# Batch 0 of a linear attention and MLP kernel: k and v with nine tokens to a partition, v cast on the core, products by quarters of the array

## The chip, the core and the metric

The kernel runs on one core of a Trainium2 chip. The core has TensorE (PE, with its weight loads listed apart as PEld), VectorE (DVE), ScalarE (ACT), GpSimd (POOL) and SyncE (SP, which here only issues DMAs). The metric is device time in microseconds (us); lower is better.

## What is computed

Eight batches of eight heads, 576 tokens, head size 64, all float32:

```
q_s = softmax(q, over the 64 features)
k_s = softmax(k, over the 576 tokens)
kv  = k_s^T v                      # 64 x 64 per head
x   = q_s kv                       # heads joined: 576 x 512 per batch
out = x + relu(norm(x) * g @ w1) @ w2      # norm: layer norm, w1 512 x 2048, w2 2048 x 512
```

## The kernel before

The order of all engines is written out by hand: instructions run on each engine in the order in which the program emits them. `first_batch` (L947) sets up batch 0. After it a list of main steps (TensorE's products of the MLP) is walked by `run` (L829); side work of other batches is hung in at a position counted in units of 512 columns of product, so `(2, ...)` comes after four main steps of weight 0.5.

Batches are handled one after the other: c = 0 with plain products (`mm1_part` L497 gives `ph`, `mm2_stream` L537 gives `pc`), c = 1 to 7 with a seven-product scheme (`prod1` L729, `prod` L574), and a ninth pass for the last 64 tokens of all batches. While batch c runs through the MLP, the attention of later batches is prepared beside it; their loads are issued by `load_batch` (L1067, on SP) and `load_behind` (L1057, on POOL).

Batch 0, before its first `ph` product, goes like this:

- Loads. SP issues two of q's four token groups (`load_q0`, L960) and then four DMAs of k, two heads each (L970). A partition holds six tokens of a head, so 576 tokens fill 96 partitions (`T0 = 6`, `P0 = 96`). POOL waits with a small copy into `gate` (L994) until q's first half has landed; then it issues three DMAs of v, which cast to bf16 on the way (L996), two of q's other half (L999), and the weights (L1003, L99, L103), later q and k of batch 1 (L121). The tiles that k and v of batch 0 use are handed on to later tiles: k's exps share a buffer with k of batch 1, v with `hs`.
- q. ScalarE takes exp of the first two token groups (`exp_qt` L206), VectorE sums, inverts and scales (`norm_q` L910), TensorE transposes (`eq_pT` L935, in `pe_T` L915) and VectorE copies the transposed tile `eqT` out of PSUM (L924).
- k. ScalarE takes exp pair by pair of heads (`exp_k0` L279). TensorE sums over tokens by six products with a column of ones (`z0_mm` L291), VectorE inverts (`recip_z` L301).
- kv. `kv0_mm` (L306) takes six 128-wide products for two heads at once, of which only the two diagonal 64 x 64 blocks are wanted. VectorE scales the result by the inverse sums, masks it with `diag` and sums each row (L312). The row sums, times -1/512, are spread over a 128 x 128 tile `mbc` by ScalarE (L317) or, for the last pair, VectorE (L321): it subtracts the mean of x when it is multiplied by `eqT`.
- x, transposed and with its mean taken off, comes straight from TensorE: `xT_mm` (L325) multiplies `kv_sb` and `mbc` by `eqT` for token groups 0 and 1; `xT_out` (L338) scales by g, on VectorE for columns 0 and 1, on ScalarE for 2 and 3.
- The third and fourth token groups take exp and transposing in between (L1029 to L1040: `eq_pT(0, 2)` copied by ScalarE, `eq_pT(0, 3)` by VectorE); their row sums are taken by `z_q` (L926, tile `zs`) after the first four `ph` products (L1102).

`warm` (L843) multiplies a zero tile, only to keep TensorE busy: 34 times at the start, 11 times between the two transposes.

Products on part of the array stand already in two places: `kv_pairs` (L347, k^T v of batches 1 to 7, output halves of 64 partitions) and the ninth pass (L395, 64 x 64 blocks in all four quarters).

Of the kernel before, what the change touches and what calls it, by code (L numbers as in the profile page):

```python
# [12 lines left out]
FP32 = mybir.dt.float32  # L13
# [7 lines left out]
def kernel(  # L21
# [31 lines left out]
    C9 = B  # L53
    FAST = 1
    CAST = (1, 2, 3)
    T0 = 6
    P0 = S // T0
    assert SR == 64 and B % 2 == 0

    const = ctx.enter_context(tc.tile_pool(name="const", bufs=1))  # L60
# [10 lines left out]

    ident = const.tile([P, P], BF16)
    eps_ln = const.tile([P, 1], FP32)
    gate = const.tile([P, 4], FP32)
# [4 lines left out]
    ones_w = const.tile([P, P], BF16)  # L79
    diag = const.tile([P, P], FP32)  # L80
    mbc = const.tile([P, NP, P], BF16)
# [9 lines left out]
    vr = const.tile([P, 2, H, VW], BF16)  # L91
    vm = const.tile([P, 2, T, H, VW], BF16)

    w1_src = moe_w_ch1.rearrange("(ko ki) n -> ki ko n", ki=P)
    w2_src = moe_w_ch2.rearrange("(ko ki) n -> ki ko n", ki=P)

# [180 lines left out]
    kvbox = {}  # L277

    def exp_k0(j):  # L279
        hs = slice(2 * j, 2 * j + 2)  # L280
        if j == 0:
            eks[0] = raw.tile([P, T0, H, D], BF16, tag="kt", name="ek0", bufs=1)
        nc.scalar.activation(
            eks[0][0:P0, :, hs, :].rearrange("p t h d -> p h t d"), raws[0][0][0:P0, hs], AF.Exp
        )

    def k0_mm(j, t):
        hs = slice(2 * j, 2 * j + 2)
        return eks[0][0:P0, t, hs, :], raws["v0"][0:P0, hs, t, :], P

    def z0_mm(j):  # L291

        if j == 0:
            kvbox["z0"] = mm_ps.tile([P, NP], FP32, tag="m", name="z0")
        for t in range(T0):
            nc.tensor.matmul(
                kvbox["z0"][:, j : j + 1], k0_mm(j, t)[0], ones[0:P0],
                start=(j == 0 and t == 0), stop=(t == T0 - 1), skip_group_check=True,
            )

    def recip_z():  # L301
        kvbox["rz"] = sml.tile([P, NP], FP32, tag="rzk", name="rzk")
        kvbox["sum"] = sml.tile([P, NP], FP32, tag="lnv", name="kvs")
        nc.vector.reciprocal(kvbox["rz"], kvbox["z0"])

    def kv0_mm(j):  # L306
        pool, tag = (att_ps, "a") if j < 2 else (mm_ps, "m")
        pkv = pool.tile([P, P], FP32, tag=tag, name="pkv")
        for t in range(T0):
            lhsT, rhs, w = k0_mm(j, t)  # L310
            nc.tensor.matmul(pkv[:, 0:w], lhsT, rhs, start=(t == 0), stop=(t == T0 - 1))
        nc.vector.scalar_tensor_tensor(  # L312
            kv_sb[:, 0, j, :], in0=pkv, scalar=kvbox["rz"][:, j : j + 1], in1=diag,
            op0=ALU.mult, op1=ALU.mult, accum_out=kvbox["sum"][:, j : j + 1],
        )
        if j < NP - 1:
            nc.scalar.activation(  # L317
                mbc[:, j], ones_w, AF.Copy, scale=kvbox["sum"][:, j : j + 1]
            )
        else:  # L320
            nc.vector.tensor_scalar_mul(  # L321
                out=mbc[:, j], in0=ones_w, scalar1=kvbox["sum"][:, j : j + 1]
            )

    def xT_mm(j, kh):  # L325

        if j == 0:
            pobox["T", kh] = mm_ps.tile([P, 2, 2, P], FP32, tag="m", name="pxT")
        ops = [(kv_sb[:, 0, j, :], j % 2)] if j // 2 == kh else []
        ops += [(mbc[:, j], i) for i in range(2)]  # L330
        for n, (lhsT, i) in enumerate(ops):
            nc.tensor.matmul(  # L332
                pobox["T", kh][:, i], lhsT, eqTs[0][:, 0:2, j, :],
                start=(j == 0 and n == 0), stop=(j == NP - 1 and n >= len(ops) - 2),
                skip_group_check=True,
            )

    def xT_out(i):  # L338
# [2 lines left out]
            nc.vector.tensor_scalar_mul(out=dst, in0=src, scalar1=g_one[:, i : i + 1])  # L341
        else:
            nc.scalar.activation(dst, src, AF.Copy, scale=g_one[:, i : i + 1])

    halves = (slice(0, 64), slice(64, P))

    def kv_pairs(b, ts=range(T + 1)):  # L347

# [586 lines left out]
    def eq_pT(c, t, eng):  # L935
        pe_T(eqTs[c], eqs[c][0][:, t].rearrange("p h d -> p (h d)"), t, eng)
# [10 lines left out]
    def first_batch():  # L947

        nc.scalar.preload_act_table_set("natural_log_exp_and_others")
        raws[0] = (  # L950
            mlp.tile([P, H, T0, D], FP32, tag="hT", name="kt0", bufs=1), None,
            raw.tile([P, H, T, D], FP32, tag="qt", name="qt"),
        )
        k0, _, q0 = raws[0]
        v0 = mlp.tile([P, H, T0, D], BF16, tag="hs", name="v0", bufs=1)
        raws["v0"] = v0
# [8 lines left out]
        def src0(x, h0, hn):  # L965
            return x[0, h0 : h0 + hn].rearrange("h (p t) d -> p h (t d)", t=T0)

        load_q0(0, 2, nc.sync)
        for h0 in range(0, H, 2):
            nc.sync.dma_start(  # L970
                k0[0:P0, h0 : h0 + 2].rearrange("p h t d -> p h (t d)"), src0(k, h0, 2)
            )
# [10 lines left out]
        nc.vector.memset(ones_w, -1.0 / DM)  # L983
        nc.vector.memset(diag, 0.0)
        for ps in halves:
            nc.vector.memset(diag[ps, ps], 1.0)
        nc.vector.memset(kv_sb[:, 1:B], 0.0)
        nc.vector.memset(vr, 0.0)
        for half in range(2):
            nc.vector.memset(vr[64 * half : 64 * half + 64, :, 4 * half : 4 * half + 4, D:], 1.0)  # L990
        nc.vector.memset(vm[:, :, :, :, D:], 1.0)
        make_identity(nc, ident)
        nc.gpsimd.tensor_copy(out=ident_f, in_=ident[0:KO1, 0:KO1])
        nc.gpsimd.tensor_copy(out=gate, in_=q0[:, 1, 0, 0:4])  # L994
        for h0, hn in ((0, 4), (4, 2), (6, 2)):
            nc.gpsimd.dma_start(  # L996
                v0[0:P0, h0 : h0 + hn].rearrange("p h t d -> p h (t d)"), src0(v, h0, hn)
            )
        for t in range(2, T):  # L999
            load_q0(t, 1, nc.gpsimd)  # L1000
        for kh in range(2):
            ks = slice(2 * kh, 2 * kh + 2)
            nc.gpsimd.dma_start(w1_sb[:, ks, 0:512], w1_src[:, ks, 0:512])  # L1003
        for nb in range(1, 4):
            load_w1(nb)
        load_w2(0)
        load_w2(1)

        new_eq(0)
        start_x(0)  # L1010
        warm(34)
        for t in range(2):
# [54 lines left out]
    def load_batch(b, parts=(2, 0), after=None):  # L1067

        alloc(b, parts)
        for which in parts:  # L1070
            if after is None:
                nc.vector.memset(raws[b][which][0:1, 0, 0, 0:1], 0.0)
            else:
                nc.gpsimd.tensor_copy(out=raws[b][which][0:1, 0, 0, 0:4], in_=after)
        for which in parts:
            hn = H // 2 if (b, which) == (B - 1, 2) else H
            for h0 in range(0, H, hn):
                load_main(nc.sync, b, which, h0, hn)
        if 0 in parts:
            load_krem(nc.sync, b)  # L1080
# [104 lines left out]
```

## Time and profile before

| what | us |
|---|---|
| median of 3 runs | 264.61 (262.91 to 264.71) |
| the profiled execution | 263.19 |
| its span, first to last instruction | 261.4 |
| granted TensorE clock in it | 0.999 of full |
| k of batch 0: last exp starts | 9.46 |
| first `ph` product starts | 15.17 |
| first `zs` product starts | 15.61 |

The profile is of one execution. Times in it count from the start of the span. "TENSOR_TENSOR eq<-eq,rq 128x512" is an instruction that writes tile eq from eq and rq; L913 is the line of the kernel. In the timeline and the chain the first number is the start and the second the duration; in square brackets stand the idle time before it and what ended that. In a table by stretches, each engine has its busy time and in brackets its count of instructions, then come granted clock, DMA share and GB/s. A DMA that casts is counted there by the bytes that it writes.

### The profile page before, as it was taken

How to read it: one execution, taken by the hardware profiler on the slowest of the kernel's cores; microseconds unless marked ns; L12 is line 12 of the kernel's file. 1: busy time of each engine (PE TensorE's matmuls, PEld its weight loads, DVE VectorE, ACT ScalarE, POOL GpSimd, SP SyncE). 2: the span in 40 equal slices, each digit the busy share in tenths (PEclk: the TensorE clock that was granted, in tenths of full speed). 3: DMA queues.
4: the chain of work that ended last, by engine and by line, in shares of the span. 5: the costliest groups of instructions: out<-in, count | busy, mean ns of one | idle time of the engine just before them, and what ended most of it. 6: DMA issues, size and time to landing. Idle time of an engine off the chain costs nothing.

```text
span 261.4 us, 6802 instructions
## 1 busy us (share of the span) xinstructions
PE 255.1 (98%) x2667; PEld 219.9 (84%) x2667; DVE 223.9 (86%) x505; ACT 176.7 (68%) x348; POOL 94.4 (36%) x148
## 2 busy tenths in 40 slices
PE   8899999999999999999999999999999999999993
PEld 6789755788888998899889889988898888888883
DVE  6778996989999999899889988998898979977873
ACT  4657780997887785789478947894789277538400
POOL 3962228414059205920881088009100800030000
PEclk9999999999999999999999999999999999999999
DMA  7999999989999994999399938995905323221014
GB/s 195 253 206 207 356 215 276 290 192 285 171 143 277 274 174 33 294 264 115 84 263 263 154 79 290 245 153 130 266 4 111 112 102 44 43 104 56 3 41 120
DMA packets 82616, 45.00 MB, mean 172 GB/s; under 512 B 58196, under 2 KB 79192, under 8 KB 82584
## 3 DMA queue, kind: packets, MB, share of 16 engines
q0 software_dynamic: 32464, 21.76, 44.9%
q1 hardware_dynamic: 49488, 22.29, 40.6%
q10 hardware_dynamic: 632, 0.53, 0.7%
q8 instruction: 20, 0.33, 0.5%
q14 instruction: 12, 0.10, 0.1%
HBM read 36.70 MB, written 9.44 MB: 177 GB/s over the span
## 4 chain that ended last, share of the span: by engine, by line
PE 92%; DMA 3%; DVE 2%; SPq 1%; ACT 0%; issue 0%
PE ba L589 21%; PE bx L742 20%; PE bb L742 10%; PE ph L505 8%; PE bb L589 5%; PE bc L589 5%; PE be L589 5%; PE pc L541 5%; PE bc L742 5%; PE po L404 3%; DMA kt<-in_k_dram 3%; PE pkv L361 2%; PE ptr L918 1%; PE pxT L332 1%; SPq L970 1%; DVE bb L773 0%
## 5 line engine op out<-in xcount | busy, mean ns | idle before, releaser
L589 PEld LDWEIGHTS <-hs 128*128 128x128 bf16 x512 | 49.8, 98 | 5.8
L742 PEld LDWEIGHTS <-w_raw 128*128 128x128 bf16 x480 | 45.5, 98 | 5.2
L259 POOL TENSOR_TENSOR tq<-xnT 128x256 bf16<-128x256 bf16 x26 | 16.8, 665 | 73.7 <-DMA xnT<-xn 49.5
L589 PEld LDWEIGHTS <-hT 128*128 128x128 bf16 x392 | 37.4, 98 | 4.2
L742 PEld LDWEIGHTS <-w1g 128*128 128x128 bf16 x360 | 34.3, 98 | 4.3 <-issue 0.3
L742 PE MATMUL bx<-tq,w_raw 128*128 128x256 bf16 x240 | 31.6, 273 | 0.0
L589 PE MATMUL ba<-w_q,hs 128*128 128x256 bf16 x256 | 30.8, 273 | 0.0
L766 ACT COPY bc<-bx 128x512 f32<-128x512 f32 x30 | 16.6, 594 | 19.0 <-PE bx L742 19.0
L773 DVE TENSOR_TENSOR bb<-bx,s 128x512 f32<-128x512 f32 x30 | 19.5, 694 | 8.2 <-ACT s L770 5.5
L607 POOL DMA_DIRECT2D out_dram<-ot x28 | 15.5, 559 | 23.7 <-DVE ot L601 23.6
L784 ACT ACTIVATE hT<-bb 128x512 bf16<-128x512 f32 x30 | 16.3, 595 | 10.8 <-PE bb L742 10.8
L417 ACT ACTIVATE scrap<-x,mv 128x512 bf16<-128x512 bf16 x32 | 23.1, 722 | 0.3
L784 ACT ACTIVATE hT<-bc 128x512 bf16<-128x512 f32 x30 | 16.3, 594 | 8.9 <-PE bc L742 8.9
L572 DVE TENSOR_TENSOR hs<-hT 128x1024 bf16<-128x1024 bf16 x32 | 21.7, 685 | 0.5 <-ACT hT L784 0.5
L404 PE MATMUL po<-kv_sb,eqT 128*128 128x128 bf16 x128 | 22.0, 219 | 0.0
L776 DVE TENSOR_TENSOR hT<-bx,s 128x512 bf16<-128x512 f32 x30 | 19.3, 683 | 3.1 <-PE bx L742 3.1
L449 DVE SCALAR_TENSOR_TENSOR x<-po,rq 128x512 bf16<-128x512 f32 x30 | 20.5, 683 | 0.9 <-PE po L404 0.8
L218 DVE TENSOR_REDUCE zq<-eq 128x16 f32<-128x1024 bf16 (+1 forms) x20 | 20.8, 1050 | 0.5 <-ACT eq L209 0.5
L615 ACT COPY s<-ba 128x512 f32<-128x512 f32 x15 | 8.8, 585 | 14.7 <-PE ba L589 9.7
L784 ACT ACTIVATE hT<-bx 128x512 bf16<-128x512 f32 x30 | 16.4, 602 | 0.7 <-PE bx L742 0.6
L589 PE MATMUL ba<-w_sb,hT 128*128 128x256 bf16 x128 | 16.6, 273 | 0.0
L770 ACT COPY s<-bb 128x512 f32<-128x512 f32 x30 | 16.6, 622 | 0.0
(157 smaller groups left out, 553.5 us busy)
## 6 DMA issues: line engine op xcount, KB each, us to landing
out_dram<-ot POOLq DMA_DIRECT2D x30, 256.0 KB, 6.4
kt<-in_k_dram SPq DMA_DIRECT2D x5, 1024.0 KB, 12.3
qt<-in_q_dram SPq DMA_DIRECT2D x4, 1024.0 KB, 5.9
qt<-in_q_dram POOLq DMA_DIRECT2D x2, 1024.0 KB, 12.5
kt<-in_k_dram POOLq DMA_DIRECT2D x2, 1024.0 KB, 13.7
vm<-in_v_dram POOLq DMA_DIRECT2D x16, 128.0 KB, 11.1
qt<-in_q_dram SPq DMA_DIRECT2D x3, 512.0 KB, 4.7
w_raw<-in_moe_w_ch_dram POOLq DMA_DIRECT2D x3, 512.0 KB, 10.3
```

Source lines behind the costliest of these rows:

```text
L218: nc.vector.reduce_sum(eqs[c][1][:, ts], eqs[c][0][:, ts], axis=AX.X)
L259: eng.tensor_tensor(out=dst[:, t], in0=x[:, t], in1=y[:, t], op=ALU.subtract)
L404: nc.tensor.matmul(pobox["p"][:, i * P : i * P + P], eqTs[c][:, t, i, :], kv_sb[:, c, i, :], start=True, stop=True,)
L417: nc.scalar.activation(scrap, x[:, t], AF.Square, bias=mv[:, t, 0:1], scale=-float(DM), accum_out=mv[:, t, 1:2],)
L449: nc.vector.scalar_tensor_tensor(x[:, t].rearrange("p (h d) -> p h d", h=H), in0=pobox[c, t].rearrange("p (h d) -> p h d", h=H), scalar=1. ...
L505: nc.tensor.matmul(ph[:, m % 2, at : at + tn], (w1g if c else w1_sb)[:, ko, m * P : (m + 1) * P], xnTs[c][:, t0 : t0 + tn, ko, :], start=( ...
L572: nc.vector.tensor_tensor(out=dst, in0=x, in1=y, op=op)
L589: nc.tensor.matmul(hbox[bank][:, t, cs], lhsT, rhs[:, cs], start=first and (own or t == 0) and k == 0, stop=k == KH - 1, skip_group_check= ...
L742: nc.tensor.matmul(dst[:, q], lhsT, rhs, start=first and q == 0 and ko == 0, stop=ko == 1, skip_group_check=True)
L773: nc.vector.tensor_tensor(out=at[g, "b"], in0=at[g, "x"], in1=at[g, "s"], op=ALU.add)
L776: nc.vector.tensor_tensor(out=h_out(g, 1, 1), in0=at[g, "x"], in1=at[g, "s"], op=ALU.add)
L784: nc.scalar.activation(h_out(g, odd, half), at[g, name], AF.Relu)
```

## The change

- k and v of batch 0 are laid out with nine tokens to a partition: a pair of heads takes 128 partitions, the lower 64 for the even head and the upper 64 for the odd one. A DMA of a pair has 128 runs of 2304 B.
- Both are loaded as float32 by SP, v right behind k, in four DMAs each; then SP loads q's other half in one DMA. POOL issues neither v nor q any more. VectorE casts v to bf16, pair by pair (`cast_v0`). The float32 v takes the second buffer of the tag that q of batches 0 and 1 uses.
- POOL's `gate` waits for k's last DMA instead of q's first. The zero fill of `kv_sb` for batches 1 to 7 moves from VectorE to POOL; VectorE fills that of batch 0.
- Sums and k^T v are taken by products on diagonal quarters of the array: 18 of 64 x 64 per pair for each, into two PSUM tiles. VectorE scales and sums the lower half, ScalarE the upper one. `diag`, `ones_w` and `mbc` go; VectorE makes one column `kvm` per pair, which `xT_mm` takes as a broadcast 128 x 128 operand.
- Four fill products come after each pair's sums (`warm(4)`), and the order of kv, xT and q's other half changes: `exp_qt` of groups 2 and 3 and both `eq_pT` now stand behind most of xT, and ScalarE's `xT_out` ahead of its copy of `eqT`.
- q and k of batches 6 and 7 are loaded in two halves each (before, only q of batch 7).

```diff
-    T0 = 6
-    P0 = S // T0
+    T0 = 9
...
+    ones_f = const.tile([P, D], FP32)
+    kvm = const.tile([P, NP], BF16)
...
     def exp_k0(j):
...
+            eks[0] = raw.tile([P, NP, T0, D], BF16, tag="kt", name="ek0", bufs=1)
+        nc.scalar.activation(eks[0][:, j], raws[0][0][:, j], AF.Exp)
...
+            kvbox["z0"] = [mm_ps.tile([P, NP], FP32, tag="m", name="z0") for _ in halves]
         for t in range(T0):
+            for z0, ps in zip(kvbox["z0"], halves):
+                nc.tensor.matmul(
+                    z0[ps, j : j + 1], eks[0][ps, j, t], ones[ps],
+                    start=(j == 0 and t == 0), stop=(t == T0 - 1), skip_group_check=True,
+                )
...
+        for z0, ps in zip(kvbox["z0"], halves):
+            nc.vector.reciprocal(kvbox["rz"][ps], z0[ps])
+
+    def cast_v0(j):
+        nc.vector.tensor_copy(out=raws["v0"][:, j], in_=raws["v0f"][:, j])
...
     def kv0_mm(j):
...
         for t in range(T0):
+            for pk, ps in zip(pkv, halves):
+                nc.tensor.matmul(
+                    pk[ps], eks[0][ps, j, t], raws["v0"][ps, j, t],
+                    start=(t == 0), stop=(t == T0 - 1),
+                )
+        rz, total = [kvbox[name][:, j : j + 1] for name in ("rz", "sum")]
+        lo, hi = halves
         nc.vector.scalar_tensor_tensor(
+            kv_sb[lo, 0, j, lo], in0=pkv[0][lo], scalar=rz[lo], in1=ones_f[lo],
+            op0=ALU.mult, op1=ALU.mult, accum_out=total[lo],
+        )
+        nc.scalar.activation(
+            kv_sb[hi, 0, j, hi], pkv[1][hi], AF.Copy, scale=rz[hi], accum_out=total[hi]
+        )
+        nc.vector.tensor_scalar_mul(out=kvm[:, j : j + 1], in0=total, scalar1=-1.0 / DM)
...
-        ops += [(mbc[:, j], i) for i in range(2)]
+        ops += [(kvm[:, j : j + 1].to_broadcast([P, P]), i) for i in range(2)]
...
+        def src0(x, j0, jn):
+            heads = x[0, 2 * j0 : 2 * (j0 + jn)]
+            return heads.rearrange("(j two) (s t) d -> (two s) j (t d)", two=2, t=T0)
...
         load_q0(0, 2, nc.sync)
+        for x, dst in ((k, k0), (v, v0f)):
+            for j in range(NP):
+                nc.sync.dma_start(
+                    dst[:, j : j + 1].rearrange("p j t d -> p j (t d)"), src0(x, j, 1)
+                )
+        load_q0(2, 2, nc.sync)
...
-        nc.vector.memset(kv_sb[:, 1:B], 0.0)
+        nc.vector.memset(kv_sb[:, 0], 0.0)
+        nc.gpsimd.memset(kv_sb[:, 1:B], 0.0)
+        nc.gpsimd.tensor_copy(out=gate, in_=k0[:, NP - 1, 0, 0:4])
...
         for j in range(NP):
             exp_k0(j)
             z0_mm(j)
+            cast_v0(j)
+            warm(4)
             if j == NP - 2:
                 g_columns()
         recip_z()
         kv0_mm(0)
         kv0_mm(1)
+        xT_mm(0, 0)
+        xT_mm(0, 1)
         kv0_mm(2)
-        xT_mm(0, 0)
+        xT_mm(1, 0)
+        xT_mm(1, 1)
         kv0_mm(3)
-        exp_qt(0, 2)
-        exp_qt(0, 3)
-        xT_mm(1, 0)
         xT_mm(2, 0)
-        xT_mm(0, 1)
+        xT_mm(2, 1)
         xT_mm(3, 0)
         xT_out(0)
         xT_out(1)
-        eq_pT(0, 2, nc.scalar)
-        xT_mm(1, 1)
-        xT_mm(2, 1)
-        eq_pT(0, 3, nc.vector)
+        exp_qt(0, 2)
+        exp_qt(0, 3)
         xT_mm(3, 1)
         xT_out(2)
         xT_out(3)
+        eq_pT(0, 2, nc.scalar)
+        eq_pT(0, 3, nc.vector)
...
-            hn = H // 2 if (b, which) == (B - 1, 2) else H
+            hn = H // 2 if b >= B - 2 else H
```

More of the change, by code (lines that the diff above doesn't have):

```diff
@@ L73 @@
     eps_ln = const.tile([P, 1], FP32)
-    gate = const.tile([P, 4], FP32)
     ones = const.tile([P, 1], BF16)
@@ L78 @@
     bones = const.tile([P, 2], BF16)
-    ones_w = const.tile([P, P], BF16)
-    diag = const.tile([P, P], FP32)
-    mbc = const.tile([P, NP, P], BF16)
+    ones_f = const.tile([P, D], FP32)
+    gate = const.tile([P, 4], FP32)
+    kvm = const.tile([P, NP], BF16)
     g_one = const.tile([P, KO1], FP32)
@@ L92 @@
     vm = const.tile([P, 2, T, H, VW], BF16)
+    halves = (slice(0, 64), slice(64, P))
     w1_src = moe_w_ch1.rearrange("(ko ki) n -> ki ko n", ki=P)
@@ L279, in exp_k0 @@
     def exp_k0(j):
-        hs = slice(2 * j, 2 * j + 2)
         if j == 0:
[L282 to L289, printed above, removed]
+            eks[0] = raw.tile([P, NP, T0, D], BF16, tag="kt", name="ek0", bufs=1)
+        nc.scalar.activation(eks[0][:, j], raws[0][0][:, j], AF.Exp)
     def z0_mm(j):
         if j == 0:
-            kvbox["z0"] = mm_ps.tile([P, NP], FP32, tag="m", name="z0")
+            kvbox["z0"] = [mm_ps.tile([P, NP], FP32, tag="m", name="z0") for _ in halves]
         for t in range(T0):
[L296 to L299, printed above, removed]
+            for z0, ps in zip(kvbox["z0"], halves):
[3 more added lines that the diff above has]
+                )
     def recip_z():
@@ L303, in recip_z @@
         kvbox["sum"] = sml.tile([P, NP], FP32, tag="lnv", name="kvs")
-        nc.vector.reciprocal(kvbox["rz"], kvbox["z0"])
+        for z0, ps in zip(kvbox["z0"], halves):
+            nc.vector.reciprocal(kvbox["rz"][ps], z0[ps])
+    def cast_v0(j):
+        nc.vector.tensor_copy(out=raws["v0"][:, j], in_=raws["v0f"][:, j])
     def kv0_mm(j):
-        pool, tag = (att_ps, "a") if j < 2 else (mm_ps, "m")
-        pkv = pool.tile([P, P], FP32, tag=tag, name="pkv")
+        pkv = [
+            pool.tile([P, D], FP32, tag=tag, name="pkv")
+            for pool, tag in ((att_ps, "a"), (mm_ps, "m"))
+        ]
         for t in range(T0):
-            lhsT, rhs, w = k0_mm(j, t)
-            nc.tensor.matmul(pkv[:, 0:w], lhsT, rhs, start=(t == 0), stop=(t == T0 - 1))
+            for pk, ps in zip(pkv, halves):
[5 more added lines that the diff above has]
+        lo, hi = halves
         nc.vector.scalar_tensor_tensor(
-            kv_sb[:, 0, j, :], in0=pkv, scalar=kvbox["rz"][:, j : j + 1], in1=diag,
-            op0=ALU.mult, op1=ALU.mult, accum_out=kvbox["sum"][:, j : j + 1],
-        )
[L316 to L323, printed above, removed]
+            kv_sb[lo, 0, j, lo], in0=pkv[0][lo], scalar=rz[lo], in1=ones_f[lo],
+            op0=ALU.mult, op1=ALU.mult, accum_out=total[lo],
+        )
+        nc.scalar.activation(
+            kv_sb[hi, 0, j, hi], pkv[1][hi], AF.Copy, scale=rz[hi], accum_out=total[hi]
+        )
+        nc.vector.tensor_scalar_mul(out=kvm[:, j : j + 1], in0=total, scalar1=-1.0 / DM)
     def xT_mm(j, kh):
@@ L343, in xT_out @@
             nc.scalar.activation(dst, src, AF.Copy, scale=g_one[:, i : i + 1])
-    halves = (slice(0, 64), slice(64, P))
     def kv_pairs(b, ts=range(T + 1)):
@@ L950, in first_batch @@
         raws[0] = (
-            mlp.tile([P, H, T0, D], FP32, tag="hT", name="kt0", bufs=1), None,
+            mlp.tile([P, NP, T0, D], FP32, tag="hT", name="kt0", bufs=1), None,
             raw.tile([P, H, T, D], FP32, tag="qt", name="qt"),
@@ L954, in first_batch @@
         k0, _, q0 = raws[0]
-        v0 = mlp.tile([P, H, T0, D], BF16, tag="hs", name="v0", bufs=1)
-        raws["v0"] = v0
+        v0 = mlp.tile([P, NP, T0, D], BF16, tag="hs", name="v0", bufs=1)
+        v0f = raw.tile([P, NP, T0, D], FP32, tag="qt", name="v0f")
+        raws["v0"], raws["v0f"] = v0, v0f
         def load_q0(t, tn, eng):
@@ L963, in load_q0 @@
             )
-        def src0(x, h0, hn):
-            return x[0, h0 : h0 + hn].rearrange("h (p t) d -> p h (t d)", t=T0)
+        def src0(x, j0, jn):
+            heads = x[0, 2 * j0 : 2 * (j0 + jn)]
+            return heads.rearrange("(j two) (s t) d -> (two s) j (t d)", two=2, t=T0)
         load_q0(0, 2, nc.sync)
[L969 to L972, printed above, removed]
+        for x, dst in ((k, k0), (v, v0f)):
[4 more added lines that the diff above has]
+        load_q0(2, 2, nc.sync)
         raws["g"] = outp.tile([KO1, P], FP32, tag="ot", name="g_rows")
@@ L982, in first_batch @@
         nc.vector.memset(bones[64:P, 1:2], 1.0)
[L983 to L986, printed above, removed]
-        nc.vector.memset(kv_sb[:, 1:B], 0.0)
+        nc.vector.memset(ones_f, 1.0)
+        nc.vector.memset(kv_sb[:, 0], 0.0)
+        make_identity(nc, ident)
+        nc.gpsimd.tensor_copy(out=ident_f, in_=ident[0:KO1, 0:KO1])
+        nc.gpsimd.memset(kv_sb[:, 1:B], 0.0)
+        nc.gpsimd.tensor_copy(out=gate, in_=k0[:, NP - 1, 0, 0:4])
         nc.vector.memset(vr, 0.0)
@@ L991, in first_batch @@
         nc.vector.memset(vm[:, :, :, :, D:], 1.0)
[L992 to L1000, printed above, removed]
         for kh in range(2):
```

## The prediction

> **What bounds the kernel now.** I read the page's busy shares and chain first, then the chain of waits over the first 45 us, then the timeline of the first 20 us, then the stretches of one us for the DMA rate.
>
> ```profile
> span 261.4 us, 6802 instructions
> PE 255.1 (98%) x2667; PEld 219.9 (84%) x2667; DVE 223.9 (86%) x505; ACT 176.7 (68%) x348; POOL 94.4 (36%) x148
> ...
> PE 92%; DMA 3%; DVE 2%; SPq 1%; ACT 0%; issue 0%
> ```
>
> TensorE is 98% busy and is 92% of the chain that ended last. The 3% of DMA is one piece, batch 0's k:
>
> ```profile
> 2.85 6.59 DMA kt<-in_k_dram
> ...
> 9.46 0.85 ACT ek L283
> ...
> 10.66 0.37 PE pkv L311 x6
> ...
> 13.62 0.39 PE pxT L332 x2
> ...
> 15.33 0.44 PE ph L505 x4
> 15.77 0.08 PE zs L930 x4
> ```
>
> Up to 15 us the chain goes from k's landing through exp, sums, k^T v and the folded product to the first `ph` product; from there TensorE leads almost alone (112 `ph` products take 11.37 us, later 16 take 1.75 us: 102 and 109 ns each). So nothing behind 15.6 us gives time back: what the first stage loses or wins reaches the end one for one. Three engines set that stage:
>
> ```profile
> 8.18 0.69 DVE L913 TENSOR_TENSOR eq<-eq,rq 128x512 bf16<-128x512 bf16 x1
> 8.93 0.40 PE L918 MATMUL ptr<-ident,eq 128*128 128x128 bf16 x4
> 9.36 0.42 DVE L924 COPY eqT<-ptr 128x512 bf16<-128x512 bf16 x1 [0.15 <-PE ptr L918]
> ...
> 14.27 0.59 ACT L920 COPY eqT<-ptr 128x512 bf16<-128x512 bf16 x1 [0.17 <-PE ptr L918]
> ...
> 15.37 0.84 ACT L343 ACTIVATE xnT<-pxT,g_one 128x256 bf16<-128x256 f32 x2 [0.51 <-PE pxT L332]
> ```
>
> VectorE's q chain (unchanged) holds TensorE until 8.93 and VectorE until 9.78. ScalarE makes q's transposed third quarter at 14.27, before its two `xnT` copies at 15.37. The rate of the loads:
>
> ```profile
> 3.00:4.00 1.00, 1.00 (x6) 0.69 (x5) 0.95 (x1) 0.00 (x0) 0.00 (x0) 1.00 1.13 340
> 4.00:5.00 1.00, 1.00 (x7) 0.71 (x5) 0.88 (x1) 0.00 (x0) 0.00 (x0) 1.00 1.15 368
> ...
> 6.00:7.00 1.00, 0.85 (x8) 0.51 (x6) 0.93 (x3) 0.92 (x2) 1.00 (x2) 1.00 1.09 264
> 7.00:8.00 1.00, 0.63 (x8) 0.60 (x9) 0.97 (x3) 0.79 (x1) 1.00 (x2) 1.00 1.08 256
> ```
>
> The last column is GB/s: 340 to 368 while q's 128 partitions arrive, 256 to 264 while k's 96 do.
>
> **The loads.** k becomes 128 partitions of 2304 B runs. Rate between 262 (k's now) and 368; I take 368, the row with 128 partitions in it. Counting bytes, q's first half is in by 4.06; exp then starts at 5.00, so a landing is seen 0.95 us after its last byte. k (1.18 MB, 3.2 us) is in by 7.3, seen 8.2 (now 9.46); v, now twice the bytes in SBUF, by 10.5, seen 11.4; q's other half (0.52 MB at 340) by 12.0, seen 13.0. At 262 v is seen at 14.0. SP's extra issues take 0.5 us each and end by about 6, ahead of the data: nothing. POOL loses v's 2.14 us and q's 1.88 us of issuing, but its gate now waits for k's last piece: w1 is issued from about 8.4 instead of 9.09. Its first product is now at 15.17, later below: nothing.
>
> **Moved setup.** The zero fill of kv_sb leaves VectorE (1.55 us at 2.40, in a stretch that ends in its wait for q at 5.66: no gain). On POOL it costs 1.55 (VectorE's row) to 5.7 us (28 times ident's 0.20); from 1.6 us on that ends before the gate opens. Later batches' halved loads are three more SP issues of 0.5 us, hidden since SP waits 14 us at a time for xn; if not, 0.5 us on a transpose.
>
> **VectorE's cast.** Four of 128x576 f32 to bf16. No such row: 0.24 each by the 128x1024 bf16 copy (0.43), 0.75 by the f32 clamp (0.68 for 512). I take 0.46, from the 0.42 of the 512-wide copy, nearest in size and not f32-slow. In order behind 9.78: three casts, g's two small ops (0.31), the last cast: 11.9 (13.1 at 0.75). TensorE's sums come later (below), so the casts are hidden; at 262 GB/s the last v makes it 14.5, and they aren't.
>
> **Quarter products.** 18 per pair of heads for z and 18 for k^T v instead of 6 each. Cheapest row: C9's 64x64 products, 32 in 0.38 us, 12 ns. Dearest: today's z, 18 in 0.59, 33 ns. Nearest, since two tiles of the array take turns: kv_pairs, 40 in 0.76, 19 ns. Entering and leaving them costs something too:
>
> ```profile
> 81.64 0.76 PE pkv L361 x40
> 82.40 1.85 PE bx L742 x16
> ...
> 108.94 1.75 PE bx L742 x16
> ```
>
> The 16 products behind them took 0.10 more. So a group of 18 is 0.34 + 0.10 = 0.44 (0.22 to 0.70). Fill: four products of 0.109 = 0.44 per pair; three of these lie before the last z.
>
> [...]
>
> **TensorE's timeline.** It is free at 9.16. Four z groups 1.76, three fills 1.31, g 0.2: 12.43, read at 12.55. (All exps of k are done by then.) Two reciprocals at 0.18: 12.9. Last fill and kv0(0): 13.31, readable 13.46. Each pair then needs ScalarE's scaled half (0.31 by the rows of L343 and L317, read of the accumulator 0.20) and VectorE's kvm (0.15 by its one-column row), 0.05 of signals: 0.7 us, against 0.37 + 0.41 to 0.50 now. xT(0) ends at 14.64; kv0(2) 15.08; xT(1), five products, 15.63; kv0(3) 16.07, readable 16.22; xT(2) 16.62; kvm(3) is ready at 16.93, xT(3) 16.97 to 17.52. Its first product is now at 13.62: 3.35 later.
>
> **The new order on ScalarE.** After its half of pair 3 (16.73) come both exps of q (1.15 by the pair at 5.00: 17.88), then both xT_out (0.84: 18.74), only then the copy of eqT (0.59: 19.33). TensorE, in order, transposes by 18.15, does four `ph` (18.2 to 18.65, now 15.17) and waits for that copy: zs at 19.4, now 15.61. **Sum: 3.8 us later**, and `ph` behind it follows.
>
> The profiled execution took 263.19 us (span 261.4, 1.8 around it), 1.4 below the median of 264.61 shown. 263.2 + 3.8 = 267.0; on the median 268.4; I forecast between, 267.8.
>
> **Rivals.**
> - Cheap products: 12 ns, no switching, casts of 0.35. z ends at 11.5, kv0(3) is readable at 14.5, ScalarE's row from 14.95 ends at 17.5: 1.9 us later, 265.8. For: C9's rows. Against: there four tiles take turns, here two.
> - Dear products or late v. At 33 ns with 0.10 switching, z ends at 13.5, kv0(3) is readable at 18.1, zs at 21.4: 5.8 later, 269.7. v at 262 GB/s: last cast 14.5, first scaling 14.9 instead of 13.46: 5.2 later, 269.1. For: z's row now; k's rate now. Against: kv_pairs; 340 to 368 with 128 partitions.
> [...]
> - Not slower: the landing of k is the only gate. k is seen 1.2 to 1.5 us earlier; if all behind it kept today's distance (9.46 to 15.17), the time would be 262.6. It decides if z, cast and kv0 are done 1.4 us behind k's last piece, as now. Against: v's last byte is 3.2 us behind k's, and VectorE is not free for casts before 9.78. Faster still would need a gain behind 15 us, where no row waits for what changes.
>
> **How the numbers follow.** Forecast (2.7 to 4.9 later) 0.54; cheap products 0.20; dear products or late v 0.13; drains 0.05; not slower 0.08. Leaving out a tenth at either end: from 264.5 (between not slower and cheap products) to 270.6 (dear ends on the median). Within 1% (2.65 us, about what a measurement of this kernel tells from no change) lie cheap products, most of not slower and a little of the forecast: 0.30; faster by over 1%: 0.05; slower: 0.65.
>
> **What would show it.** Right: z's last product near 12.4, the reciprocals behind TensorE rather than behind the cast, zs near 19.4 waiting for ScalarE's eqT copy, and later stages unchanged in length. Wrong in a step: groups of 18 far from 0.44; the last cast ending after z; k seen at 9.4 still; a granted clock under 1.00 or warm products over 109 ns in the stage. A time at or below 264 would refute the one-for-one passage to the end, or the timeline.

## The result, and the profile after

The changed kernel takes 267.13 us (median of 4 runs, 267.1 to 267.83); the kernel before, run beside it, 264.56 (4 runs, 262.91 to 264.71). The ratio is 1.0118, with a 95% interval of 1.0075 to 1.0161: slower by about 1.2%. The forecast was 267.8, with a range of 264.5 to 270.6. The profiled execution took 267.17 us, 3.98 more than that of before (263.19); its span grew by 4.0, from 261.4 to 265.4, and the granted clock is 0.999 in both. Two of the 87 executions of the kernel before that stand beside the experiments below, with spans of 264.5 and 265.3, count as slow and are left out.

The page's head of the kernel after, with its busy shares:

```profile
span 265.4 us, 7047 instructions
...
PE 258.7 (97%) x2776; PEld 221.8 (84%) x2779; DVE 223.7 (84%) x510; ACT 176.1 (66%) x353; POOL 93.6 (35%) x144
```

TensorE is still the bound, and is busy for 3.6 us more than before. The difference has to be looked for in the chain (start, duration, engine and tile):

```profile
9.28 0.37 PE z L289 x18
9.66 0.54 PE warm L846 x4
...
13.26 0.45 PE pkv L311 x18
...
18.11 0.84 ACT xnT L344 x2
18.95 0.48 ACT eqT L919
...
19.48 0.27 PE zs L929 x4
...
46.00 0.76 PE pkv L360 x40
...
260.88 0.46 PE bf L588 x8
```

What the reader is to see: from 9.28 on the chain is no longer k's landing but TensorE itself: sums and fill by turns, four times 0.91 us with g's product (0.31) ahead of the last. From 13.26 to 18.11 the chain goes to and fro between TensorE and the scaling of `kv_sb` and `kvm` on ScalarE and VectorE. It ends in ScalarE's two `xnT` and its `eqT` copy, and `zs` starts at 19.48 instead of 15.61, 3.87 later. In the kernel before, the last two of these rows stand at

```profile
42.12 0.76 PE pkv L361 x40
...
256.89 0.46 PE bf L589 x8
```

so the distance is 3.88 at 46 us and 3.99 at the end: 240 us of kernel behind the first stage add 0.1 us. All of the difference between these two executions is made before 19.5 us.

From the timeline of the kernel after (in brackets the idle time before, and what ended it), the landing of k as POOL's gate sees it, the last cast with g's copy ahead of it, and the reciprocals:

```profile
8.00 0.19 POOL L991 COPY gate<-kt 128x4 f32<-128x4 f32 x1 [3.43 <-DMA kt<-in_k_dram]
...
12.38 0.16 DVE L943 COPY g_one<-gcp 128x4 f32<-128x4 f32 x1 [0.85 <-PE gcp L942]
12.53 0.48 DVE L301 CAST v<-v0f 128x576 bf16<-128x576 f32 x1
12.93 0.37 DVE L298 RECIPROCAL rzk<-z 64x4 f32<-64x4 f32 x2
```

k is there at 8.00 where it used to be seen at 9.46, and nothing comes of it: its last sums are ready 4.7 us later. The stretches of 6 to 8 us show why it came early (the last column is GB/s):

```profile
6.00:7.00 1.00, 0.96 (x9) 0.60 (x7) 0.93 (x3) 1.00 (x3) 0.00 (x0) 1.00 1.07 401
7.00:8.00 1.00, 0.67 (x9) 0.63 (x9) 0.97 (x3) 0.94 (x3) 0.00 (x0) 1.00 1.04 387
```

With k on 128 partitions the loads run at 387 to 401 GB/s, where they ran at 256 to 264 with 96. These two executions lie far apart: over all profiles, the stretch from 6 to 7 us has 264 to 306 with 96 partitions (six profiles) and 320 to 401 with 128 (eight).

### The profile page after: what moved, and what is told of

Read it like the earlier page. It is cut to its first block, busy times and chain, and to the rows that moved or that the text cites. A ratio compares the mean times of both kernels' runs of the same rounds, so it can differ in the third digit from the quotient of the medians.

```text
span 265.4 us, 7047 instructions
## 1 busy us (share of the span) xinstructions
PE 258.7 (97%) x2776; PEld 221.8 (84%) x2779; DVE 223.7 (84%) x510; ACT 176.1 (66%) x353; POOL 93.6 (35%) x144
## 4 chain that ended last, share of the span: by engine, by line
PE 94%; DMA 2%; DVE 1%; ACT 1%; issue 0%; DVEq 0%
PE ba L588 21%; PE bx L741 20%; PE bb L741 10%; PE ph L504 7%; PE bb L588 5%; PE bc L588 5%; PE be L588 5%; PE pc L540 5%; PE bc L741 5%; PE po L403 3%; PE pkv L360 2%; DMA qt<-in_q_dram 2%; PE ptr L917 1%; PE warm L846 1%; PE pxT L333 1%; PE z L289 1%
## 5 line engine op out<-in xcount | busy, mean ns | idle before, releaser
L772 DVE TENSOR_TENSOR bb<-bx,s 128x512 f32<-128x512 f32 x30 | 19.4, 694 | 8.6 <-ACT s L769 5.6
## 6 DMA issues: line engine op xcount, KB each, us to landing
kt<-in_k_dram SPq DMA_DIRECT2D x3, 1024.0 KB, 11.7
```

The costliest lines, as they stand in the source:

```text
L772: nc.vector.tensor_tensor(out=at[g, "b"], in0=at[g, "x"], in1=at[g, "s"], op=ALU.add)
```

## The experiments

Each kernel ran beside the kernel before on the same chip. Its span is compared with the 265.2 to 265.4 of the changed kernel's runs, or with the spans of before, whose spread is a question of its own below. Spans are used because the time around them varies (1.7 to 3.2 us). Where the start of `zs` is compared, it is its start in the timeline; in a chain the same products can stand up to 0.2 us later, because the pieces of a chain don't overlap.

### The fill products left out

```diff
             cast_v0(j)
-            warm(4)
```

> The changed kernel without the four fill products after each pair's sums. Theory (the fill lies on TensorE's path): z's last product ends near 11.0 instead of 12.7, and then VectorE's last cast, near 12.3, sets the reciprocals; the first scaling starts at 12.7 instead of 13.7, zs at 18.5 instead of 19.48, span about 1.0 us shorter (264.4). Rival 1 (the fill fills idle time; v's landing or its cast sets the stage already): span within 0.2 us of 265.4. Rival 2 (without fill the clock falls): warm or ph products over 109 ns and a longer span.

Measured: 266.55 us (265.17 to 267.45, 10 runs), 1.0098 of before (1.0070 to 1.0125). Three of the ten executions, at a full clock, have spans of 263.4 to 263.8, 1.6 to 2.0 below the changed kernel, more than the 1.0 expected. In the other seven the mean clock is 0.985 to 0.994 and the span 264.6 to 265.7. The profiled one is of these. (Its casts took 455 ns in the median, not 619, and the last one waited for v's landing at 11.27. Shorter casts may be why the gain is larger than expected where the clock holds; no profile at a full clock shows it.) Its stretches, in which the third number from the right is the granted clock:

```profile
11.00:11.50 0.50, 0.48 (x31) 0.36 (x24) 0.39 (x4) 0.00 (x0) 0.50 (x2) 1.00 1.15 291
11.50:12.00 0.50, 0.00 (x0) 0.00 (x0) 0.47 (x3) 0.00 (x0) 0.50 (x1) 0.69 1.26 282
12.00:12.50 0.50, 0.00 (x0) 0.00 (x0) 0.33 (x3) 0.35 (x3) 0.50 (x2) 0.50 1.20 205
```

The clock is halved from about 11.7 to 18.5 us. A mean of 0.69 over 11.50 to 12.00 puts the fall near 11.7, when TensorE had been idle for some 0.2 us, after 2.3 us of quarter products with g's product among them. So the first five `pxT` products take 1.25 us (0.80 in the changed kernel), and `zs` comes half a microsecond later than with the fill:

```profile
12.60 1.25 PE pxT L333 x5
...
19.93 0.27 PE zs L929 x4
```

The theory and the second rival are both borne out: the fill stands on the path, and without it the mean clock is lower in seven of ten executions, which takes most of the gain back. In the profiled execution TensorE's whole idle stretch was about 1.1 us (11.47 to 12.60), and the clock fell at the beginning of it. Whether the quarter products ahead of it or the idle time brought the clock down, no run shows.

### Half of the fill

```diff
-            warm(4)
+            warm(2)
```

> The changed kernel with two fill products per pair instead of four. Theory (each fill product takes its 0.11 us of TensorE's path until VectorE's last cast sets the stage, and the clock holds while TensorE has work): 8 products fewer, of which 0.65 to 0.9 us show: zs near 18.7, span near 264.5, granted clock 1.00. Rival (the clock needs all four): clock under 0.997 in some executions, as without any fill, and a spread of over 1 us.

Measured: 266.84 us (266.15 to 267.68, 4 runs), 1.0113 (1.0073 to 1.0154). The chain of the profiled execution, which kept its clock:

```profile
18.62 0.27 PE zs L929 x4
```

`zs` is 0.86 earlier: four groups of 0.32 instead of 0.54. The span, 264.4, is 1.0 shorter. The fill is on the path product for product. In two of the four executions the mean clock was 0.993 and 0.994 and the spans 265.4 and 265.9, so half of the fill doesn't hold the clock safely.

### ScalarE's copy of eqT ahead of its last two xT

```diff
+        eq_pT(0, 2, nc.scalar)
         xT_mm(3, 1)
         xT_out(2)
         xT_out(3)
-        eq_pT(0, 2, nc.scalar)
         eq_pT(0, 3, nc.vector)
```

> The changed kernel with the transposes of q's third quarter and ScalarE's copy of them ahead of ScalarE's two xT_out. Theory (the order on ScalarE makes zs wait): zs starts near 18.75 instead of 19.48 and the span is 0.7 us shorter (264.7). Rival (the wait only moves: xT_out comes later and the second half of the first ph products waits instead): zs earlier but span within 0.2 us of 265.4.

Measured: 266.89 us (266.32 to 267.82, 4 runs), 1.0110 (1.0068 to 1.0152); spans of 264.4 to 264.8, some 0.8 below the changed kernel. The end of the stage in the timeline:

```profile
18.50 0.60 PE L504 MATMUL ph<-xnT,w_raw 128*128 128x256 bf16 x4
18.93 0.24 PE L929 MATMUL zs<-bones,eqT 128*128 128x2 bf16 x4
```

`zs` no longer waits for ScalarE; it comes when TensorE gets there, 0.55 earlier, and the `pkv` group at 46.00 comes 0.55 earlier too (45.45). The forecast 18.75 was missed by 0.18, of which 0.1 is that TensorE entered `pkv` at 13.36 instead of 13.26. The step was real and small: a seventh of the 3.87 at `zs`, a fifth of the loss by the spans.

### The fill in the kernel before

```diff
             z0_mm(j)
+            warm(4)
```

> The kernel before with four fill products after each pair's sums: one part of the change alone. Theory (fill lies on TensorE's path unless a wait covers it): z's last group ends at about 11.3 instead of 10.66, covered only in part by the wait for k until 10.36; zs 0.6 to 0.9 us later than 15.61, span 262.0 to 262.3. Rival (covered by the wait for k): span 261.4 as before.

Measured: 264.7 us (264.5 to 264.91, 10 runs), 1.0029 (1.0011 to 1.0047). The profiled span is 262.8, 1.4 over the profiled one of before, where 0.6 to 0.9 was expected:

```profile
11.53 0.46 PE warm L847 x4
11.99 0.35 PE pkv L311 x6
```

The expectation had forgotten the last fill: it stands ahead of the first `pkv`, which now starts at 11.99 instead of 10.66. `zs` came at 17.12, 1.51 later. So the fill alone, without a new layout, carries over a third of the loss.

### q's other half late, in the kernel before

```diff
         kv0_mm(3)
-        exp_qt(0, 2)
-        exp_qt(0, 3)
...
-        eq_pT(0, 2, nc.scalar)
         xT_mm(1, 1)
         xT_mm(2, 1)
-        eq_pT(0, 3, nc.vector)
+        exp_qt(0, 2)
+        exp_qt(0, 3)
         xT_mm(3, 1)
         xT_out(2)
         xT_out(3)
+        eq_pT(0, 2, nc.scalar)
+        eq_pT(0, 3, nc.vector)
```

> The kernel before with the changed kernel's place for q's other half alone: both exps behind the last xT but one, both transposes and ScalarE's copy of eqT behind ScalarE's two xT_out. Theory (the order on ScalarE costs by itself): zs starts 0.6 to 0.9 us later than 15.61, at 16.2 to 16.5, and the span grows as much. Rival (in the kernel before, q lands too late for an earlier place to matter): zs within 0.2 us of 15.61.

Measured: 264.94 us (263.32 to 266.33, 10 runs), 1.0036 (1.0006 to 1.0067). Its timeline:

```profile
15.47 0.60 PE L505 MATMUL ph<-xnT,w_raw 128*128 128x256 bf16 x4
...
16.60 0.25 PE L930 MATMUL zs<-bones,eqT 128*128 128x2 bf16 x4 [0.52 <-ACT eqT L920]
```

`zs` waits for ScalarE's copy as in the changed kernel and starts 0.99 later than before, just past the expected 16.2 to 16.5. But this execution also has v landing at 11.82, behind which `pkv` waited. The first `ph` starts 0.30 later than before (15.17); from there to `zs` it is 1.13 instead of 0.44. So about 0.3 of the 0.99 is v's lateness and about 0.7 the order's, as expected. The span, 263.5, is 2.1 over the profiled one of before: 0.94 of it is there when VectorE starts its last write (258.32, before 257.38), the rest lies behind that write. The spans run from 261.4 to 264.5, with a median about 1.2 over that of before on the same chip.

### The loads of later batches as before

```diff
-            hn = H // 2 if b >= B - 2 else H
+            hn = H // 2 if (b, which) == (B - 1, 2) else H
```

> The changed kernel with q and k of batches 6 and 7 loaded as before (only q of batch 7 in halves). Theory (hidden): span 265.2 to 265.4 as in the changed kernel, the stages of the last three batches unchanged in length. Rival (the halves delay SP's transposes or bring exps forward): a difference of 0.5 us or more in those stages.

Measured: 268.05 us (267.78 to 268.68, 4 runs), 1.0161 (1.0123 to 1.0199); spans of 265.4 to 265.5 and `zs` at 19.54. The spans are those of the changed kernel, so the halved loads are hidden, as the prediction had it; the higher median lies in the time around the span.

### No fill, and v cast by ScalarE

```diff
     def cast_v0(j):
-        nc.vector.tensor_copy(out=raws["v0"][:, j], in_=raws["v0f"][:, j])
+        nc.scalar.copy(raws["v0"][:, j], raws["v0f"][:, j])
...
             z0_mm(j)
-            cast_v0(j)
-            warm(4)
...
+        for j in range(NP):
+            cast_v0(j)
         recip_z()
```

> The changed kernel without fill and with v cast by ScalarE after k's exps instead of by VectorE. Theory (without fill VectorE's casts are the next limit): reciprocals end near 11.4, ScalarE's first half starts near 11.7 (behind its last cast), zs at 17.4 and the span 2.0 us shorter than 265.4. Rival (TensorE's products alone set it): same as without fill alone. Rival (v lands late): ScalarE waits for v and the first scaling starts after 12.5.

Measured: 265.32 us (264.97 to 267.64, 10 runs), 1.0068 (1.0039 to 1.0098); six executions at a full clock have spans of 263.2 to 263.6, the others, at 0.985 to 0.994, 264.3 to 265.9. The profiled one came as expected, `zs` at 17.41:

```profile
10.97 0.63 ACT v L301
...
17.41 0.27 PE zs L929 x4
```

With the fill gone and VectorE free, v's landing at 10.94 leads the chain. ScalarE's row of two exps, two `xnT` and the copy then sets the end, the row that the prediction named. About half of the loss is given back. v's last piece now comes 1.5 us behind the time at which k used to be there; how the rest is shared between that and ScalarE's row, this run doesn't show.

### A new order around the same layout

Sums of three pairs take the place of the 11 warm products between q's transposes, with two fill products behind each. Two casts and the last go to ScalarE, one stays on VectorE. The scaling is parted from the products (`kv0_out`), q's exps come right behind the last of it, and VectorE makes both copies of `eqT`.

```diff
         eq_pT(0, 0, nc.vector)
-        warm(11)
-        eq_pT(0, 1, nc.vector)
-        for j in range(NP):
+        for j in range(3):
             exp_k0(j)
             z0_mm(j)
-            cast_v0(j)
-            warm(4)
-            if j == NP - 2:
-                g_columns()
+            warm(2)
+        eq_pT(0, 1, nc.vector)
+        exp_k0(3)
+        cast_v0(0, nc.scalar)
+        cast_v0(1, nc.scalar)
+        z0_mm(3)
...
+        kv0_out(3)
+        exp_qt(0, 2)
+        exp_qt(0, 3)
...
+        eq_pT(0, 2, nc.vector)
         xT_out(2)
         xT_out(3)
-        eq_pT(0, 2, nc.scalar)
         eq_pT(0, 3, nc.vector)
```

> The changed kernel's loads and quarter products in another order: z of three pairs takes the place of the fill between the two transposes of q, two casts of v go to ScalarE after k's exps and one behind VectorE's first scaling, products of k^T v stand ahead of their scaling, q's other half before the last xT, its copies on VectorE; four fill products per pair become two in four places. Theory (the layout is not what costs: the place of z, fill, casts and copies is): z ends near 9.6, the reciprocals near 10.1, kv0(3) waits for v's last piece (10.9) and its cast, ph starts near 14.3 and zs near 14.8, both about 0.8 us earlier than in the kernel before; span 260.5 to 261.0 with the clock at 1.00. Rival (the layout costs by its later v): ph starts after 15.2 and the span is not below 261.4. Rival (clock): falls in some executions, spans of 262 and more.

Measured: 264.12 us (263.8 to 265.13, 12 runs), 1.0002 (0.9978 to 1.0026); spans of 262.0 to 263.3. `zs` came at 16.55, and the expected 14.8 was missed by 1.75 us. Three groups of sums with fill took 2.10 us (7.89 to 9.99), where the 11 warm products had taken 1.20, so q's second transpose slipped from 8.93 to 9.99. The first rival's signs came (`ph` at 16.08, no span below 261.4), but not its cause: neither v's landing nor a cast stands in the chain from 8 us to `zs`. All the same, the loss is gone by the medians: layout, casts and quarter products are in it, and it runs like the kernel before. By the profiled spans 1.0 of the 4.0 is left.

The same without those three fills, and with g's product ahead of the first transpose:

```diff
         for t in range(2):
             exp_qt(0, t)
             norm_q(0, t)
+        g_mm()
         eq_pT(0, 0, nc.vector)
         for j in range(3):
             exp_k0(j)
             z0_mm(j)
-            warm(2)
...
-        g_mm()
```

> The reordered kernel (z of three pairs between q's two transposes) with its three pairs of fill products there taken out and g's product moved ahead of the first transpose; one pair of fill products stays, behind k^T v of the second pair. Theory (TensorE's own products were its path: three fill groups of 0.33 us and g's 0.31 in front of z's last group): z ends 1.2 us earlier, near 9.4, and zs starts between 15.1 and 15.5 instead of 16.55 (15.61 in the kernel before); span near 261.2. Rival (v's last piece and its cast take over): zs no earlier than 15.9. Rival (clock): without that fill the clock falls in some executions, granted mean under 0.995 and spans above 262.4.

Measured: 264.2 us (263.43 to 264.91, 12 runs), 0.9993 (0.9971 to 1.0016); spans of 261.6 to 263.1. Both rivals came true. The cast of v's last piece, in the chain:

```profile
11.36 0.67 ACT v L302
```

Now v's last piece, seen at 11.33, and its cast lead; the first `zs` is at 16.11, half a microsecond behind the kernel before. Five of the twelve executions had a mean clock of 0.994, with spans of 262.6 to 263.0. So the layout doesn't have to cost anything, but no order tried here makes it gain: what k gives, v takes.

### The kernel before, looked at again

The profiles differ by 4.0 us and the medians by 2.6. Over its runs beside the experiments the kernel before has spans from 260.7 to 264.1, with a median of 262.1 (85 executions), at full clock for the most part; the profiled one, at 261.4, is a short one. The changed kernel stays within 265.2 to 265.4. The first guess was that the landings of the first stage make the spread. The same kernel, one more profile:

> The kernel before once more, for a second trace of it. Theory (its first stage is set by landings, which differ from execution to execution: spans of 260.7 to 263.7 in its runs): if the span differs by 0.5 us or more from 261.4, the difference lies before zs, in a wait of TensorE or ScalarE for k or v, and the stages behind zs have the same length within 0.1 us. Rival: the stages behind zs differ.

Measured: 265.05 us, span 263.3, clock 1.0: a long one. But `zs` starts at 15.49, no later than in the short one (15.61), and at 50 us the two differ by 0.2. The guess fell. The rest comes here:

```profile
69.50 7.67 DMA xnT<-xn
...
77.34 1.30 POOL tq L259 x2
```

The DMA transpose of batch 2's `xn` landed at 77.2. POOL's differences, which need it, started at 77.34 (74.56 in the first profile), and TensorE ran dry, waiting 1.3 us for them: it was 1.40 and 1.10 us busy of 2.00 in the two stretches from 76 to 80. Further back, POOL's copy that lets the load of batch 3's q go (timeline of this execution):

```profile
59.03 0.18 POOL L1074 CAST qt<-eqT 1x4 f32<-1x4 bf16 x1 [5.52 <-DMA eqT<-eq]
```

It waits for another DMA transpose, batch 2's `eqT`, and came 1.2 us later than in the first profile (57.80). Batch 3's loads followed, and they stand ahead of the transposes of `xn`. Is it these loads? Two kernels ask it, one with the loads later, one with q's load freed from that wait.

Loads later, waiting for `kv_sb` of batch 2:

```diff
-        s += [(10, lambda: load_batch(3, (2,), eqTs[2][0:1, T - 1, NP - 1, 0:4])), (37, lambda: load_batch(3, (0,)))]
+        s += [(40.5, lambda: load_batch(3, (2,), kv_sb[0:1, 2, 0, 0:4])), (40.7, lambda: load_batch(3, (0,)))]
...
-        s += [(10.1, lambda: load_v(3))]
+        s += [(40.6, lambda: load_v(3))]
```

> The kernel before, with only this moved: the load of q of batch 3 (and with it v's and k's) waits for kv_sb of batch 2, ready about 59.5 us, instead of for the transposed eqT of batch 2, which landed at 57.8 in the first trace of before and at 59.0 in the second. All engines' other work keeps its place. Theory (the spread of before comes from these loads: where they are issued over a microsecond later, the transposes of xn of batch 2 that stand behind them on the queue land too late, and TensorE idles about 1.5 us near 77 us): every execution is now like the long ones of before, loads issued at 59.0 to 60.0, the wait near 77 us in the profile, spans 262.8 to 264 with few under 262.5, median about 1 us over that of before. Rival (the transposes are late for another reason, the loads' place is only a companion): the same spread and median as before, spans from 261.

Measured: 266.34 us (264.61 to 267.99, 11 runs), 1.0074 (1.0040 to 1.0107); spans of 262.8 to 266.2, median 264.1, beside 261.1 to 263.9 of before on the same chip.

```profile
70.25 7.96 DMA xnT<-xn
```

The gate's copy came at 59.91. The late loads make the long span: every execution is now at or over 262.8, and the late transpose stands in the chain. POOL's differences start at 78.37, and TensorE waits 1.6 us for them. Not all of this execution's 3.0 us over the first profile of before is that wait. Its first `ph` waited for w1, which landed at 15.68, and started at 15.72 instead of 15.17; at 43 us it was 0.84 late, and the other 2.14 came between 58 and 85 us.

Loads freed:

```diff
-        s += [(10, lambda: load_batch(3, (2,), eqTs[2][0:1, T - 1, NP - 1, 0:4])), (37, lambda: load_batch(3, (0,)))]
+        s += [(10, lambda: load_batch(3, (2,))), (37, lambda: load_batch(3, (0,)))]
```

> The kernel before, with the load of q of batch 3 freed from its wait for the transposed eqT of batch 2: it is issued as soon as its buffer is free, near 54 us instead of 57.8 to 59.0. Theory (late loads hold the transposes of xn): the loads are done some 4 us earlier, those transposes land in time in every execution, spans 260.7 to 261.8 with none near 263, median 0.5 to 1 us under that of before. Rival 1 (lateness has another cause): spread as before. Rival 2 (the wait is there for a reason: the early load runs beside the transposes of eqT of batch 2 and makes those late): the first x products of batch 2, near 60 us, wait, and the spans are 263 or more.

Measured: 264.11 us (263.18 to 265.59, 12 runs), 0.9993 (0.9966 to 1.0020); spans of 261.2 to 262.7. None of 12 reaches 263, where 5 of the 20 of before beside it do, and the transposes of `xn` land 5.0 us after their issue (median of two), instead of 6.6 in the first execution of before and 8.6 in the long one. With so few executions none over 263 could also be chance; that later loads make the wait rests on the kernel with the late gate. The median hardly moved, against the expectation, and the load came not 4 us earlier but right behind the transpose of `eqT` on its queue. What is left of the spread shows in the profiled execution, of 262.7:

```profile
5.11 6.81 DMA v<-in_v_dram
```

v landed at 11.92, the first `pkv` started at 11.96 instead of 10.66, `zs` at 16.80 instead of 15.61: 1.2 us, and the span is 1.3 longer. So the spread of the kernel before has sources that were seen: late transposes of batch 2, by the loads ahead of them, late landings of v, and, in the kernel with the late gate, a late landing of w1.

In the changed kernel v's landing is covered by TensorE's sums and fill (12.72). Its loads of batch 3 were in time in its one profile: q was issued 0.6 us behind the start of TensorE's `pkv` group near 60 us, where it was 0.4 in the first profile of before, 1.5 in the second and 1.7 with the late gate, and the transposes landed 6.4, 6.6, 8.6 and 8.8 us after their issue. Why that held in all of the eight executions that have this first stage (spans 265.2 to 265.5) is not settled. It is not the new layout: the kernel before with fill has no long span in ten executions either (262.7 to 263.1).

## Why the prediction was right, step by step

- **One for one to the end.** Right between the two profiled executions: 3.87 at `zs`, 3.88 at 46 us, 4.0 at the end. As a statement on the kernel before it was too strong. In some of its executions there is a wait near 77 us that the one profile didn't show. That wait, and late landings, make its median span 262.1, 0.7 over the execution that the sum was made from. This is why the medians differ by less than the sum.
- **The sum.** 3.8 predicted at `zs`, 3.87 measured. Counted on the profiled execution it gave 267.0, and 267.17 came; the forecast of 267.8, moved halfway to the median, was 0.7 over the median of 267.13. The move rested on the median of three runs; counted straight, the sum was nearer. That the straight sum met the median too has some luck in it: the execution it was counted from was 0.7 shorter than the median span, while the changed kernel's spans hardly vary; by the medians the kernel lost 2.6, not 3.8.
- **Quarter products and fill.** Predicted 0.44 for each, with 0.10 of switching put on the sums. Measured: sums 0.37, fill 0.54, together 0.91 for 0.88. The switching is there, but it shows in the rows of the fill behind (a fill of the same four products takes 0.46 in the kernel before). At 0.54, a fill product takes 135 ns at a full clock; over 109 was named as a sign that a step is wrong, and here the misplaced 0.10 is that step. The last sums end at 12.72, predicted 12.43.
- **Drains.** No run shows the term behind the chance of 0.05 for drains. What the runs showed in its place: a group of sums and its fill took 0.91 us. In the timeline of the kernel after, weight loads wait 0.21 us ahead of the second and third group of sums, beside fill products that still run. Sums and fill by turns cost about 0.1 us a group: without fill three groups of sums take 1.01 together, 0.34 each, and with 0.46 for four fill products in the kernel before with fill that is 0.80.
- **The casts.** Predicted 0.46 each, hidden behind the sums. All casts of the kernel after:

```profile
L301 DVE CAST v<-v0f x4: 451/619/819, 9.7 to 12.5; 128x576 bf16<-128x576 f32 x4
```

  The median is 0.62. More than the size, the order was off: g's two copies stand ahead of the last cast and wait for `gcp` until 12.38, so that cast ends at 13.0, behind the last sums (12.72). The prediction had named this as a sign that a step is wrong, and it was: the reciprocals came behind the cast, not behind TensorE. They started at 12.93, by the forecast at 12.55. The products, held by the fill until 13.26, didn't suffer. Without the fill the last cast does lead to the reciprocals in the chain, there behind v's landing.
- **kv and xT.** First `pkv` readable 13.71 (13.46), last xT ending 17.87 (17.52): the lateness entered ahead of it and was carried on.
- **ScalarE's row.** Exps, `xnT`, copy, then `zs` at 19.4: measured 19.48, waiting for that copy. With the copy moved ahead the wait goes and `zs` comes 0.55 earlier, so TensorE's own path was right behind it.
- **The loads.** k seen at 8.2: 8.00 measured. The rate taken, 368 GB/s, was low; 387 to 401 came. "Not slower" fell as its condition said: it asked for sums, cast and `pkv` 1.4 us behind k, and they came 5.7 behind.
- **Moved setup.** The zero fill on POOL took 3.07 us, within 1.55 to 5.7, and ended at 4.57, ahead of the gate. The halved loads are hidden, as their removal shows.
- **Where the loss lies.** By single edits: the fill 1.6 to 2.0 us of the changed kernel's span, in the executions that keep their clock; the copy's place 0.55 at `zs` and about 0.8 by the spans; fill and casts on VectorE together, about 1.9 at a full clock. They overlap and are not to be added. The new orders, in which layout and quarter products stay and most casts move to ScalarE, have the time of before by the medians, and by the profiled spans the last one keeps 0.4 of the 4.0. So most of the loss is one of order, fill and the engine of the casts, not of the layout.

## What to carry to other kernels

An earlier landing is worth only what the engines behind it can take up: here k came 1.5 us earlier, and what was put behind it (products, fill, casts and their order) cost 5.3. Before fill products are taken out or put in, look at the granted clock in stretches of half a microsecond over several executions; they were on the path here, and without them the mean clock was lower in 7 of 10 executions, and in 4 of 10 with the casts on ScalarE. And a sum made from one profiled execution is as good as that execution is typical: look at the spread of spans first, and where a waiting DMA decides it, count on a wait that the profile at hand doesn't show.

## What the runs showed of the hardware that was not expected

- In the one such execution that was profiled, the clock halved for 6.8 us after 2.3 us of mostly 64 x 64 products, when TensorE had been idle for some 0.2 us. Mean clocks of 0.994 and less show a loss in 7 of 10 executions without fill and in 2 of 4 with half of it; with all of it the mean clock was 0.997 or more in 12 of 12. The kernel before has 0.994 or less in 6 of 85.
- From 6 to 7 us, loads of k and v ran at 320 to 401 GB/s on 128 partitions (eight profiles), loads of k at 264 to 306 on 96 (six). The runs grew from 1536 to 2304 B as well; the two were not told apart. Short runs alone were not slow, though: q's, of about 520 B by its packets (650 for 0.34 MB from 3 to 4 us), reached 340 on 128 partitions.
- 18 products on alternating diagonal quarters took 0.37 us, 21 ns each, and the full products behind them took 0.08 us more (0.54 against 0.46 for four).
- The same cast of 128x576 from float32 took 0.451 to 0.819 us within one execution.
- DMA transposes that stand behind large loads on their queue landed 5.0 to 8.8 us after their issue (median of the two of each profile): 8.6 and 8.8 where q of batch 3 was issued 1.5 and 1.7 us behind the start of TensorE's `pkv` group, 6.6 and 6.4 where that was 0.4 and 0.6. Loads 1.2 us later made TensorE wait 1.3 us some 18 us behind them; 2.1 us later, 1.6 us.
